# Retention attention and two feed-forward stages: where in the program weights are converted

## The chip, the core and the metric

The kernel runs on one core of one Trainium2 chip. What is measured is the device time of one execution in microseconds (us). The program has 17,896 profiled instructions on five engines: TensorE (PE, with its weight loads as PEld), VectorE (DVE), ScalarE (ACT), GpSimd (POOL) and SyncE (SP), which issues the transfers.

## What is computed

```python
def _attn_ref(q, k, v):                        # 4 x 8 heads, 576 positions, 64 wide
    scores = scale * np.matmul(q, k.transpose(0, 1, 3, 2))
    ret = scores * Dmat[None, :, :, :]         # gamma ** distance, causal
    return np.matmul(ret, v)

x = attn_out as 2304 tokens x 512
h = x @ w_in                                   # 512 x 2048
g = np.maximum(h, 0.0) ** 2
x = g @ w_out                                  # 2048 x 512
p = domain_probs / (domain_probs.sum(-1, keepdims=True) + 1e-09)
for e in range(4):                             # 4 experts, 512 x 1024 x 512
    h = np.maximum(x @ w1[e], 0.0)
    out += p[:, e:e + 1] * (h @ w2[e])
```

## The kernel before

**Number format.** Every float32 operand of the feed-forward stages is split into a high and a low part in a reduced float32 type, and a product is three matmuls: high by high, high by low, low by high. Making the parts is a *conversion*: ScalarE casts the high part, and another engine subtracts it for the low part. For a weight this is the helper `split` (ScalarE line 124, POOL line 125); the first stage's weights come in 64-bit floats and go through `from_f64` (lines 87 to 121), which for each piece of 128x256 runs one ScalarE operation, five on VectorE, then one on ScalarE and two on POOL.

**Chunks and groups.** The hidden width is cut into chunks c of 256. Chunks 0 to 7 belong to the dense stage (`NW1 = 8`), 8 to 23 to the experts over token groups 0, 1 and 4, and 24 to 39 to the experts again, over groups 2 and 3. Groups 0 to 3 have 512 tokens and group 4 has 256. A job is a chunk with one group or with a pair of groups. `layer1` (line 460) or `layer1_pair` (line 494) makes the hidden values of a job, `layer2_1` (line 613) or `layer2_2` (line 645) multiplies them by the second weight, one job behind. `layer1_pair` computes two groups with seven block products in place of eight: a *set* of 42 matmuls in the order A11, S2, S3, A12, S1, A22, S4, with sums on VectorE between them (line 501). Its fourth product adds to the bank of the first, and may start only when ScalarE has copied that bank (line 507).

**Input blocks.** A pair reads seven prepared input blocks (slots 0 to 6 of `xh`, `xl`). `slots` prepares them from `y` in three generators: `parts` casts a half on ScalarE (line 573) and takes the low part (line 574) of the first half on VectorE and of the second on POOL; `minus` forms differences on VectorE (line 581). Generators `sa` serve groups 0 and 1 ahead of chunk 8, `sb` serve groups 2 and 3 ahead of chunk 24.

**Banks.** All matmul results of the feed-forward stages rotate through eight PSUM banks, so a result can be started only when the one eight places earlier has been read: by line 619 on ScalarE (chunk 0), 621 on VectorE, or 653 on VectorE.

**What sets the order of the work around the change.** Each engine's instructions run in the order in which the Python code issues them. Conversions are generators in a list `work`; `tick(n)` advances the first of them by n steps, and is called in the attention (line 419), after each half of `layer1` (469) and after each tile of `layer2` (622, 656). `pace[0]` is the number of steps (line 690). `drain` runs a generator to its end where its result is needed. `queue_weights` (line 204) puts the next weights into `work` in a fixed order as their buffers come free: `split_w1` and `split_w2` of chunk c, each with two buffers. A weight of chunks 0 to 7 takes 28 steps, a later `split_w1` 12 or 11 and a later `split_w2` 4. Raw weights arrive through three buffers (`wraw`, line 43) in pieces of 256 KB; `load_piece` issues the next load when a piece has been converted, on SP's queue, which also carries the attention's inputs and the output.

The attention runs 16 units of two steps each. Steps of conversion begin in unit 3.

Of the kernel before, what the change touches and what calls it, by code (L numbers as in the profile page):

```python
# [26 lines left out]
NW1, NW2 = 8, 16  # L27
# [6 lines left out]
def tile_kernel(ctx, tc, qT, kT, kn, vn, v4d, mask, qdec, kdec, wd, w, probs, out):  # L34
    nc = tc.nc
# [165 lines left out]
    splits = {}  # L201
    free = {(f, c) for f in (split_w1, split_w2) for c in range(2)}

    def queue_weights(*place):
        free.update(place)
        while order and order[0] in free:
            f, c = order.pop(0)
            splits[f, c] = f(c)
            work.append(splits[f, c])


    def attention(a):
# [181 lines left out]
        for i, s in enumerate(steps):  # L394
            n, h = s
            nxt = steps[i + 1] if i + 1 < len(steps) else None
            un, uc = (n, 2) if h == 0 else (n + 1, 0)
            update(un, uc)
            if nxt:
                scores(nxt)  # L400
                masked(nxt)
            cs = CS[h]
            for c in cs[:-1]:
                inner(s, c)
            update(un, uc + 1)
            inner(s, cs[-1])
            for c in cs:
                if c:
                    outer(s, c)
            finish(s)  # L410
            if h == 0:
                prepare(n + 2)
            else:
                load(n + 3)
            if h == 0 and n in (1, 2, 3):
                load_piece()
            if s == (3, 0):
                queue_weights()
            tick(1 + h)

    with tc.manual_schedule():
        with ExitStack() as a:
# [18 lines left out]
        pace = [2]  # L441
# [36 lines left out]
                out=lo, in0=h, scalar=0.0, in1=f32(hi), op0=ALU.max, op1=ALU.subtract  # L478
            )

        def layer1_pair(c, ga, gb):


            w1h, w1l = w1s[c]
            (ha, la), (hb, lb) = hidden(ga), hidden(gb)
            bank = lambda: ps.tile([128, GT], F32, name="h", tag="ps")
            v = nc.vector

            def product(o, i, j, first=True):

                n = 0
                for k in range(2):
                    for a, x in ((w1h, xh_), (w1h, xl_), (w1l, xh_)):
                        nc.tensor.matmul(  # L494
                            o, a[:, i, k, :], slot(x, j)[:, k, :], start=(first and n == 0), stop=(n == 5),
                            skip_group_check=True,
                        )
                        n += 1

            def add(o, x, y):  # L500
                v.tensor_tensor(out=o, in0=x, in1=y, op=ALU.add)  # L501

            u = [tp.tile([128, GT], F32, name="r") for _ in range(2)]
            u.append(cvp.tile([128, GT], F32, name="cv_tp"))
            b1 = bank()
            product(b1, A11, 0)
            nc.scalar.copy(out=u[0], in_=b1)  # L507
            b6 = bank()
            product(b6, S2, 3)
            add(u[1], b6, u[0])  # L510
            b7 = bank()
            product(b7, S3, 2)
            add(u[2], b7, u[1])
            product(b1, A12, 4, False)
            relu_split(b1, ha[:, 0, :], la[:, 0, :])
            b5 = bank()
            product(b5, S1, 1)
            add(u[2], b5, u[2])
            product(b7, A22, 5, False)
            add(u[0], b7, u[1])  # L520
            relu_split(u[2], hb[:, 1, :], lb[:, 1, :])
            product(b5, S4, 6, False)
            add(u[1], b5, u[1])
            relu_split(u[0], ha[:, 1, :], la[:, 1, :])
            relu_split(u[1], hb[:, 0, :], lb[:, 0, :])
            gh[c, ga], gl[c, ga] = ha, la
            gh[c, gb], gl[c, gb] = hb, lb
# [37 lines left out]
                op0=ALU.mult, op1=ALU.mult,  # L565
            )

        def parts(i, src):

            for k in range(2):  # L570
                yield
                hi = slot(xh_, i)[:, k, :]
                nc.scalar.copy(out=hi, in_=src[:, k, :])
                (nc.gpsimd if k else nc.vector).tensor_tensor(
                    out=slot(xl_, i)[:, k, :], in0=src[:, k, :], in1=f32(hi), op=ALU.subtract
                )

# [5 lines left out]
        def slots(ga, gb):  # L583
# [2 lines left out]
            b11, b21 = yacc[ga][:, :2, :], yacc[ga][:, 2:, :]  # L586
            b12, b22 = yacc[gb][:, :2, :], yacc[gb][:, 2:, :]

            def first():
                yield from parts(0, b11)  # L590
                yield from minus(b11, b12, b11)
# [4 lines left out]
                yield from parts(2, b12)  # L596

            def second():
                yield from parts(4, b21)
                yield from minus(b21, b21, b11)  # L600
                yield from parts(5, b21)

            return first(), second(), parts(6, b22)

        def layer2_1(c, g):
            w2h, w2l = w2s[c]
# [24 lines left out]
        def layer2_2(c, g):  # L631
# [7 lines left out]
            for m in range(GS[g] // 128):  # L639
# [12 lines left out]
                else:  # L652
                    nc.vector.scalar_tensor_tensor(  # L653
                        out=acc, in0=o, scalar=pr[:, tt, e : e + 1], in1=acc, op0=ALU.mult, op1=ALU.add
                    )
                tick(2)
                if last:
                    nc.sync.dma_start(out=out[tt * 128 : (tt + 1) * 128, :], in_=acc)

# [25 lines left out]
        for i, job in enumerate(jobs):  # L685
# [1 line left out]
            g = scaled.get(c)  # L687
            drain(splits[split_w1, c])

            pace[0] = 6 if i < 3 else 3 if c in (p, q) else 2  # L690
            if job in ((NW1, (0, 1)), (NW1 + NW2, (2, 3))):
                drain((sa if c == NW1 else sb)[2])
            if g and gs == (0, 1):
                for k in range(KT):
                    magnitude(g, k, rest[k])
            if len(gs) > 1:
                layer1_pair(c, *gs)
            elif job == (p, (4,)):
                s = layer1(c, *gs, lambda: scale(1, mags[1]))
                rescale(1, s)  # L700
                work.insert(0, sa[0])
            else:
                layer1(c, *gs)
# [92 lines left out]
```

## Time and profile before

| | before |
|---|---|
| median of 3 runs | 1269.1 us (1267.95 to 1269.91) |
| the profiled execution | 1268.69 us, its span 1266.9 us |
| PE busy | 1231.6 us, 97% |
| PEld busy | 1031.9 us, 81% |
| VectorE, ScalarE, POOL busy | 832.1, 452.5, 537.2 us |
| granted TensorE clock, mean | 0.993 |

The span is what the trace covers, from the first to the last instruction; 1.8 us of the execution lie around it. A busy share of PE counts overlapping matmuls and so hides short idle stretches; the timeline shows these with the engine that ended each. In a group of the lines view the numbers behind the bar are the busy time, the mean duration of one instruction, and the idle time before them.

### The profile page before, as it was taken

What the parts mean: (1) busy time and instruction counts of PE and PEld (TensorE: products, weight loads), DVE (VectorE), ACT (ScalarE), POOL (GpSimd) and SP (SyncE); (2) the same over time, 40 slices, a digit from 0 to 9 for tenths busy, and PEclk for the clock granted to TensorE, in tenths of its full rate; (3) what the DMA queues carried; (4) which work ended last, traced back from release to release, by engine and by line L of the source; (5) the groups of instructions that cost most, each with busy time, mean ns of one, the idle gap of its engine ahead of it and who ended that gap; (6) DMA issues with size and microseconds to landing.
All of it is one profiled execution on the core that took longest, in us unless ns stands there. A gap on an engine that the chain in (4) does not pass through costs nothing.

```text
span 1266.9 us, 17896 instructions
## 1 busy us (share of the span) xinstructions
PE 1231.6 (97%) x6576; PEld 1031.9 (81%) x6576; DVE 832.1 (66%) x1400; ACT 452.5 (36%) x1109; POOL 537.2 (42%) x641
## 2 busy tenths in 40 slices
PE   7998999999999996999999999999989999999998
PEld 6886788888888885888888888888868888888887
DVE  3767577777777686355765675656855676767665
ACT  3544533333333334433332322323434333333330
POOL 3655545454455349323442233422353434434340
PEclk9999999999999999999999999999999999999999
DMA  9832111111111001110111111110031101111111
GB/s 326 285 105 67 42 42 42 42 50 35 41 50 44 32 1 34 50 34 34 51 42 42 34 34 50 42 42 34 17 133 51 67 34 67 43 58 51 51 42 66
DMA packets 41303, 76.31 MB, mean 60 GB/s; under 512 B 4864, under 2 KB 5888, under 8 KB 41216
## 3 DMA queue, kind: packets, MB, share of 16 engines
q1 hardware_dynamic: 40704, 74.47, 17.3%
q8 instruction: 51, 0.84, 0.3%
q10 hardware_dynamic: 512, 0.70, 0.2%
q14 instruction: 36, 0.29, 0.1%
HBM read 70.44 MB, written 4.72 MB: 59 GB/s over the span
## 4 chain that ended last, share of the span: by engine, by line
PE 59%; DMA 0%; ACT 0%; POOL 0%; issue 0%; DVE 0%; DVEq 0%; POOLq 0%; ACTq 0%
PE o L645 31%; PE h L494 24%; PE h L460 4%; DMA wraw<-w 0%; PE o L613 0%; PE sm L537 0%; POOL w1lo L125 0%; PE po L554 0%; ACT w1hi L124 0%; POOL w2lo L125 0%; ACT r L507 0%; ACT w2hi L124 0%; DVE oacc L653 0%; DVE r L501 0%; DVE cv_m L158 0%
## 5 line engine op out<-in xcount | busy, mean ns | idle before, releaser
L653 DVE SCALAR_TENSOR_TENSOR oacc<-o,pr,oacc 128x512 f32<-128x512 f32 x270 | 197.1, 744 | 41.7 <-PE o L645 41.3
L645 PE MATMUL o<-w2hi,ghi 128*128 128x512 f32 x576 | 224.5, 390 | 0.0
L645 PE MATMUL o<-w2hi,glo 128*128 128x512 f32 x576 | 224.2, 389 | 0.0
L645 PE MATMUL o<-w2lo,ghi 128*128 128x512 f32 x576 | 224.1, 389 | 0.0
L494 PE MATMUL h<-xh,w1hi 128*128 128x512 f32 x448 | 176.7, 394 | 10.9 <-ACT r L507 8.9
L125 POOL TENSOR_TENSOR w2lo<-wraw,w2hi 128x256 fp32r<-128x256 f32 x128 | 94.1, 763 | 219.0 <-ACT w2hi L124 219.0
L494 PE MATMUL h<-xh,w1lo 128*128 128x512 f32 x448 | 175.9, 393 | 1.8 <-POOL w1lo L125 1.8
L494 PE MATMUL h<-xl,w1hi 128*128 128x512 f32 x448 | 176.0, 393 | 0.0
L125 POOL TENSOR_TENSOR glo<-r,ghi 128x512 fp32r<-128x512 f32 (+1 forms) x80 | 96.2, 1203 | 148.3 <-ACT ghi L124 147.8
L460 PE MATMUL h<-xh,w1hi 128*128 128x512 f32 (+1 forms) x448 | 154.6, 345 | 3.6 <-ACT y L619 2.8
L460 PE MATMUL h<-xl,w1hi 128*128 128x512 f32 (+1 forms) x448 | 154.0, 344 | 0.0
L460 PE MATMUL h<-xh,w1lo 128*128 128x512 f32 (+1 forms) x448 | 153.9, 344 | 0.0
L125 POOL TENSOR_TENSOR w1lo<-wraw,w1hi 128x256 fp32r<-128x256 f32 x112 | 89.3, 797 | 123.0 <-ACT w1hi L124 123.0
L501 DVE TENSOR_TENSOR r<-h,r 128x512 f32<-128x512 f32 x96 | 66.4, 691 | 103.9 <-PE h L494 95.7
L645 PEld LDWEIGHTS o<-w2lo,ghi 128*128 128x128 f32 x576 | 108.1, 188 | 22.5
L645 PEld LDWEIGHTS o<-w2hi,ghi 128*128 128x128 f32 x576 | 108.2, 188 | 22.0
L645 PEld LDWEIGHTS o<-w2hi,glo 128*128 128x128 f32 x576 | 108.2, 188 | 22.0
L613 PE MATMUL o<-glo,w2hi 128*128 128x512 f32 (+1 forms) x320 | 119.0, 372 | 4.8 <-POOL glo L125 4.8
L613 PE MATMUL o<-ghi,w2hi 128*128 128x512 f32 (+1 forms) x320 | 119.0, 372 | 2.7 <-ACT y L619 1.7
L613 PE MATMUL o<-ghi,w2lo 128*128 128x512 f32 (+1 forms) x320 | 118.4, 370 | 0.0
L494 PEld LDWEIGHTS h<-xh,w1hi 128*128 128x128 f32 x448 | 85.1, 190 | 30.6 <-ACT r L507 9.7
L465 DVE TENSOR_TENSOR r<-r 128x512 f32<-128x512 f32 (+1 forms) x80 | 58.5, 731 | 76.6 <-ACT r L464 76.4
(97 smaller groups left out, 2100.2 us busy)
## 6 DMA issues: line engine op xcount, KB each, us to landing
wraw<-w SPq DMA_DIRECT2D x128, 256.0 KB, 2.7
wraw<-wd SPq DMA_DIRECT2D x64, 256.0 KB, 2.7
q_t<-qT SPq DMA_DIRECT2D x16, 288.0 KB, 4.2
out<-oacc SPq DMA_DIRECT2D x18, 256.0 KB, 2.0
kt<-kT SPq DMA_DIRECT2D x15, 288.0 KB, 5.1
v_n<-vn SPq DMA_DIRECT2D x16, 256.0 KB, 4.3
k_n<-kn SPq DMA_DIRECT2D x15, 256.0 KB, 4.8
qd<-qdec SPq DMA_DIRECT2D x4, 224.0 KB, 4.9
```

What stands on the lines that cost most here:

```text
L125: nc.gpsimd.tensor_tensor(out=lo, in0=src, in1=f32(hi), op=ALU.subtract)
L460: nc.tensor.matmul(h, wk(a, f, k), x[:, k, :], start=(n == 0), stop=(n == 3 * KT - 1))
L465: nc.vector.tensor_tensor(out=r, in0=r, in1=r, op=ALU.mult)
L494: nc.tensor.matmul(o, a[:, i, k, :], slot(x, j)[:, k, :], start=(first and n == 0), stop=(n == 5), skip_group_check=True,)
L501: v.tensor_tensor(out=o, in0=x, in1=y, op=ALU.add)
L613: nc.tensor.matmul(o, a[:, f, 128 * m : 128 * m + 128], x[:, f, :], start=(n == 0), stop=(n == 3 * FT - 1))
L645: nc.tensor.matmul(o, a[:, f, 128 * m : 128 * m + 128], x[:, f, :], start=(n == 0), stop=(n == 3 * FT - 1))
L653: nc.vector.scalar_tensor_tensor(out=acc, in0=o, scalar=pr[:, tt, e : e + 1], in1=acc, op0=ALU.mult, op1=ALU.add)
```

## The change

In the attention every step of a unit is followed by two conversion steps (one and two before), and the first three jobs no longer run at six steps a place. Three weights are *held* out of `work`: the second weight of chunk 8 and the first weight of chunk 9 until the first set has been issued, and the first weight of chunk 25 until the set of chunk 24 is about to be issued; that one is then advanced between products of this set, three steps at each of four places. The low parts of the last three slots are taken wholly on VectorE. In `layer2_2` the pace holds in place of a fixed 2, and it is 4 in the jobs of chunk 23 (`z`).

```diff
+    held = {(split_w2, NW1), (split_w1, NW1 + 1), (split_w1, NW1 + NW2 + 1)}
+
     def queue_weights(*place):
         free.update(place)
-        while order and order[0] in free:
+        while order and order[0] in free and order[0] not in held:
...
             if s == (3, 0):
                 queue_weights()
-            tick(1 + h)
+            tick(2)
...
-        def layer1_pair(c, ga, gb):
+        def layer1_pair(c, ga, gb, steps=0):
...
             product(b1, A12, 4, False)
+            tick(steps)
             relu_split(b1, ha[:, 0, :], la[:, 0, :])
             b5 = bank()
             product(b5, S1, 1)
+            tick(steps)
             add(u[2], b5, u[2])
             product(b7, A22, 5, False)
+            tick(steps)
             add(u[0], b7, u[1])
             relu_split(u[2], hb[:, 1, :], lb[:, 1, :])
             product(b5, S4, 6, False)
+            tick(steps)
...
-        def parts(i, src):
+        def parts(i, src, engines=(nc.vector, nc.gpsimd)):
...
-                (nc.gpsimd if k else nc.vector).tensor_tensor(
+                engines[k].tensor_tensor(
...
+            late = (nc.vector, nc.vector)
...
-                yield from parts(4, b21)
+                yield from parts(4, b21, late)
                 yield from minus(b21, b21, b11)
-                yield from parts(5, b21)
-
-            return first(), second(), parts(6, b22)
+                yield from parts(5, b21, late)
+
+            return first(), second(), parts(6, b22, late)
...
-                tick(2)
+                tick(pace[0])
...
-            pace[0] = 6 if i < 3 else 3 if c in (p, q) else 2
+            pace[0] = 3 if c in (p, q) else 4 if c == z else 2
...
-                layer1_pair(c, *gs)
+                if job == (NW1 + NW2, (2, 3)):
+                    held.clear()
+                    queue_weights()
+                layer1_pair(c, *gs, steps=3 if job == (NW1 + NW2, (2, 3)) else 0)
+
+                if job == (NW1, (0, 1)):
+                    held.difference_update({(split_w2, NW1), (split_w1, NW1 + 1)})
+                    queue_weights()
```

TensorE's own instructions keep their order throughout. Three places of other engines are shown as the programs list them. The changed file is longer, so its line numbers differ: ScalarE's copy is line 507 before and 509 now, `layer1_pair`'s sums 501 and 503, its relu 476 and 478, the low parts of the slots 574 and 580, their differences 581 and 587, the evictions of `layer2_2` 653 and 661.

The first place is ScalarE ahead of the first set (chunk 8, groups 0 and 1): the last hidden values of chunk 7 (`r`, `ghi`), the last slot's casts (`xh`), and the copy on which the set's fourth product waits. Before:

```order
L573 CAST xh<-y_1332 128x512 x2
L124 CAST w1hi<-wraw 128x256
L124 CAST w1hi<-cv_d 128x256
L124 CAST w1hi<-cv_m 128x256
L124 CAST w1hi<-wraw 128x256
L124 CAST w1hi<-cv_m 128x256
L507 COPY r<-h 128x512
```

Now:

```order
L579 CAST xh<-y_1359 128x512 x2
L509 COPY r<-h 128x512
L478 ACTIVATE ghi<-h 128x512
L478 ACTIVATE ghi<-cv_tp 128x512
L478 ACTIVATE ghi<-r 128x512 x2
L124 CAST w2hi<-wraw 128x256 x4
L124 CAST w1hi<-wraw 128x256
```

Five casts of chunk 9's first weight no longer stand ahead of the copy; chunk 8's second weight and chunk 9's first follow the set's last relu.

The second place is VectorE while `layer2` of chunk 22 runs over groups 0 and 1 (eight tiles, evicted to `oacc`) and the slots of groups 2 and 3 are prepared (`xl`, and `y` for the differences). Before, the first tiles:

```order
L653 SCALAR_TENSOR_TENSOR oacc_5264<-o_8474,pr,oacc_5264 128x512
L574 TENSOR_TENSOR xl<-y_1333,xh 128x512
L653 SCALAR_TENSOR_TENSOR oacc_5264<-o_8484,pr,oacc_5264 128x512
L581 TENSOR_TENSOR y_1333<-y_1334,y_1333 128x512
L653 SCALAR_TENSOR_TENSOR oacc_5264<-o_8495,pr,oacc_5264 128x512
L581 TENSOR_TENSOR y_1333<-y_1334,y_1333 128x512
L574 TENSOR_TENSOR xl<-y_1333,xh 128x512
L653 SCALAR_TENSOR_TENSOR oacc_5264<-o_8506,pr,oacc_5264 128x512
```

Now the second to the fourth tile:

```order
L661 SCALAR_TENSOR_TENSOR oacc_5240<-o_8487,pr,oacc_5240 128x512
L587 TENSOR_TENSOR y_1360<-y_1361,y_1360 128x512
L580 TENSOR_TENSOR xl<-y_1360,xh 128x512
L587 TENSOR_TENSOR y_1361<-y_1361 128x512
L661 SCALAR_TENSOR_TENSOR oacc_5240<-o_8501,pr,oacc_5240 128x512
L587 TENSOR_TENSOR y_1361<-y_1361 128x512
L587 TENSOR_TENSOR y_1360<-y_1361,y_1360 128x512 x2
L580 TENSOR_TENSOR xl<-y_1360,xh 128x512
L661 SCALAR_TENSOR_TENSOR oacc_5240<-o_8514,pr,oacc_5240 128x512
```

Between two evictions stand two to four operations of the slots, where one or two stood. Counted over the whole listing, eighteen of them now stand ahead of the seventh eviction, nine before.

The third place is VectorE in the set of chunk 24 and behind it. Before, from the set's last sum on:

```order
L501 TENSOR_TENSOR r<-h,r 128x512
L477 SCALAR_TENSOR_TENSOR glo<-r,ghi 128x512 x2
L653 SCALAR_TENSOR_TENSOR oacc_5431<-o_8821,pr,oacc_5431 128x512
L653 SCALAR_TENSOR_TENSOR oacc_5431<-o_8834,pr,oacc_5431 128x512
L158 TENSOR_TENSOR cv_m<-wraw 128x256
L158 TENSOR_TENSOR cv_d<-cv_m,wraw 128x256
L158 TENSOR_TENSOR cv_m<-wraw 128x256
L158 TENSOR_TENSOR cv_d<-wraw,cv_d 128x256
```

Now, from the low part of the set's first finished result on:

```order
L479 SCALAR_TENSOR_TENSOR glo<-h,ghi 128x512
L158 TENSOR_TENSOR cv_m<-wraw 128x256
L503 TENSOR_TENSOR cv_tp<-h,cv_tp 128x512
L158 TENSOR_TENSOR cv_d<-cv_m,wraw 128x256
L158 TENSOR_TENSOR cv_m<-wraw 128x256
L503 TENSOR_TENSOR r<-h,r 128x512
L479 SCALAR_TENSOR_TENSOR glo<-cv_tp,ghi 128x512
L158 TENSOR_TENSOR cv_d<-wraw,cv_d 128x256
L503 TENSOR_TENSOR r<-h,r 128x512
```

The four operations on chunk 25's raw weight (`cv_m`, `cv_d`) stood behind the set and the evictions that follow it, and stand now between the set's sums.

## Rows read from the trace of the kernel before

**Rows 1.** The page: busy time, share of the span and instructions of each engine.
```profile
PE 1231.6 (97%) x6576; PEld 1031.9 (81%) x6576; DVE 832.1 (66%) x1400; ACT 452.5 (36%) x1109; POOL 537.2 (42%) x641
```

**Rows 2.** The chain that ended last, in order of time: start, us, what.
```profile
513.50 5.44 PE o L613 x24
518.94 2.87 PE h L460 x24
...
532.72 9.52 PE h L494 x42
```

**Rows 3.** Timeline of PE: start, us, engine, line, names, count [idle before, who ended it].
```profile
82.84 0.50 PE L460 MATMUL h<-xh,w1hi 128*128 128x512 f32 x1 [0.84 <-DVE xl L375]
...
140.83 0.39 PE L460 MATMUL h<-xh,w1hi 128*128 128x512 f32 x1
```

**Rows 4.** Waits of PE between 82 and 141 us: total, times, longest.
```profile
PE h L460 <- ACT y L619: 2.8, 4, 0.9
```

**Rows 5.** Windows: busy us (instructions) of PE, PEld, DVE, ACT, POOL; granted clock; DMA.
```profile
135.00:139.00 4.00, 4.00 (x13) 3.10 (x12) 1.50 (x4) 2.67 (x8) 1.47 (x2) 0.57 0.02 4
...
505.00:511.00 6.00, 5.88 (x14) 4.64 (x15) 2.43 (x5) 0.67 (x2) 1.37 (x2) 0.52 0.13 44
```

**Rows 6.** Timeline of PE around the first set.
```profile
474.43 0.28 PE L613 MATMUL o<-ghi,w2hi 128*128 128x256 f32 x1
...
484.19 0.39 PE L613 MATMUL o<-ghi,w2hi 128*128 128x512 f32 x1
...
487.86 0.50 PE L613 MATMUL o<-glo,w2hi 128*128 128x512 f32 x1 [2.55 <-POOL glo L125]
...
505.12 0.80 PE L494 MATMUL h<-xh,w1hi 128*128 128x512 f32 x1 [7.51 <-ACT r L507]
...
513.34 0.39 PE L613 MATMUL o<-ghi,w2hi 128*128 128x512 f32 x1
```

**Rows 7.** Timeline of PE around the set of chunk 25.
```profile
936.07 0.39 PE L645 MATMUL o<-w2hi,ghi 128*128 128x512 f32 x1
...
955.76 0.39 PE L645 MATMUL o<-w2hi,ghi 128*128 128x512 f32 x1
```

**Rows 8.** The chain that ended last, around the set of chunk 25.
```profile
939.67 3.01 DMA wraw<-w
...
946.33 2.59 DMA wraw<-w
```

**Rows 9.** Timeline of PE in the attention, the first outer products of units 1, 4 and 15.
```profile
18.61 0.39 PE L352 MATMUL xo<-q_s,st 128*64 128x128 f32 x4
...
31.65 0.50 PE L352 MATMUL xo<-q_s,st 128*64 128x128 f32 x6
...
80.44 0.50 PE L352 MATMUL xo<-q_s,st 128*64 128x128 f32 x6
```

**Rows 10.** Timeline of POOL ahead of the first set.
```profile
483.01 1.29 POOL L125 TENSOR_TENSOR glo<-r,ghi 128x512 fp32r<-128x512 f32 x1
484.26 1.87 POOL L125 TENSOR_TENSOR w2lo<-wraw,w2hi 128x256 fp32r<-128x256 f32 x2
```

**Rows 11.** Timeline of ACT ahead of the copy that the first set waits for.
```profile
499.39 0.40 ACT L124 CAST w1hi<-wraw 128x256 fp32r<-128x256 f32 x1
...
504.49 0.58 ACT L507 COPY r<-h 128x512 f32<-128x512 f32 x1
```

**Rows 12.** Timeline: first tile of chunk 22's `layer2`, its eviction.
```profile
896.27 0.39 PE L645 MATMUL o<-w2hi,ghi 128*128 128x512 f32 x1
...
898.48 0.74 DVE L653 SCALAR_TENSOR_TENSOR oacc<-o,pr,oacc 128x512 f32<-128x512 f32 x1
```

**Rows 13.** Timeline of DVE: two low parts of slots, without and with POOL at work.
```profile
909.80 0.68 DVE L574 TENSOR_TENSOR xl<-y,xh 128x512 fp32r<-128x512 f32 x1
...
911.09 1.38 DVE L574 TENSOR_TENSOR xl<-y,xh 128x512 fp32r<-128x512 f32 x1
```

**Rows 14.** Lines view of DVE from 898 to 918 us, the slots of groups 2 and 3.
```profile
L574 DVE TENSOR_TENSOR xl<-y,xh 128x512 fp32r<-128x512 f32 x6 | 5.3, 888 | 0.4 <-ACT xh L573 0.4
```

## The prediction

> **What bounds the kernel now.** The page comes first: TensorE is busy 97% of the span, VectorE, the next, 66% [rows 1]. TensorE's instructions keep their order in this change, so the time can move only by what TensorE waits for and by its clock. Next comes the chain that ended last, which gives the undisturbed price of each block: 24 matmuls of 512 columns take 5.44 us (0.227 each), 24 of 256 columns 2.87, and a set of 42 takes 9.52 [rows 2]. Then I read the timeline for stretches that last longer than these prices say. There are three.
>
> *Place A*, the first jobs. From 82.84 to 140.83 [rows 3] 57.99 us pass; the stretch holds 192 matmuls of 512 columns (43.5 us) and 24 of 256 (2.9), 46.4 in all. Excess 11.6. The waits there are many and short, above all 2.8 us for ScalarE to read a bank (line 619) [rows 4], and the granted clock falls to its lower level, 1.2 GHz, for most of four microseconds (mean 0.57) [rows 5]. Six conversion steps at each place load VectorE, ScalarE and POOL with more than they can do beside these jobs.
>
> *Place B*, the first set. From 474.43 to 513.34 38.91 us pass [rows 6] for 90 matmuls of 512 columns and 24 of 256, 20.4 + 2.9 = 23.3. Excess 15.6. Two waits make most of it: 2.55 for POOL's low part and 7.51 for the copy of line 507 [rows 6]; behind the second the clock stands at the lower level (0.52 over 505 to 511) [rows 5].
>
> *Place C*, the set of chunk 25. From 936.07 to 955.76 [rows 7] 19.69 us pass for 54 matmuls, 12.2. Excess 7.4. The chain shows why: two loads of raw weights, 3.01 and 2.59 us, stand on the path one behind the other [rows 8].
>
> Together 34.6 us, so a kernel without any of it would stand at 1234. The sum below is made against the profiled execution, 1268.7; the median of the runs is 0.4 higher, which I neglect.
>
> **The change part by part.**
>
> *Attention, 13 more steps.* From unit 3 on, 26 steps of the attention get 2 conversion steps each, 52 in place of 39. The first weight takes 28, so 24 of the second weight's 28 are now done there and the other 4 in the first job. Two more raw pieces are loaded there, on SP's queue between the inputs; inputs are asked for three units ahead, some 13 us, which hides a load. If that lead were gone, each would cost about the 3 us of [rows 8]. The price of the steps: units 1 to 3 last (31.65 − 18.61) / 3 = 4.35 us each, units 4 to 14, with three steps in each, (80.44 − 31.65) / 11 = 4.44 [rows 9]. So three steps cost 0.09 a unit, and 13 more about 0.4. They now also stand ahead of the longer mask multiplication, and I take **+0.7**, with 0 and 2.5 as ends (2.5 is 0.19 for each of the 13, twice what a unit's three steps cost now).
>
> *Place A, pace 2.* The first three jobs' six `layer1` places and the eight tiles behind them issue 28 steps in place of 84. That is the pace of the jobs behind 140.83, where I see no wait. Eight tiles last 10.9 us (48 times 0.227), and the eight banks give ScalarE that much slack. Nothing new is late: the second chunk's first weight needs 32 steps by the sixth job and gets 52, its second weight 60 by the seventh and gets 64. I leave 0.4 of the 11.6: **−11.2** (ends −11.6 and −8; the poor end is another dip of the clock, 1.7 us, and two thirds of the 2.8 of rows 4).
>
> *Place B.* Three things leave the path. POOL begins the first of two low parts at 483.01 and then, from 484.26, does two parts of chunk 8's second weight (1.87 us) before the other [rows 10]. With that weight held, the other ends at 485.6, or 486.2 if a VectorE operation gets in between; the 2.55 becomes about 1.1 with the restart. Second, three low parts of slots (about 1.29 us each on POOL, the size of the low part in rows 10) go to VectorE, and the other parts of the second weight go too, so what ScalarE does ahead of the copy moves forward. Third, the casts from 499.39 to the copy at 504.49 go [rows 11], 5.1 us. The copy would come at 499.4 by that alone, and about 2 us sooner by the other two: I take 497.4. The set starts when the 24 matmuls ahead of it end, 484.19 [rows 6] + 5.4 + 1.1 = 490.7, and its fourth product is due 18 matmuls (4.1) later, at 494.8. So it waits 2.6 for the copy. Next in line is VectorE: three evictions and two moved low parts stand ahead of the set's sums, and the sixth product waits for them; I put one low part, 0.7. From 474.43 to 484.19 [rows 6] pass 1.4 us more than the 8.3 that the 48 matmuls need, which nothing touches. So the residue is 1.1 + 2.6 + 0.7 + 1.4 = 5.8, and the excess falls by **−9.8** (ends −13, where the copy is in time, and −5, where it comes at 499.4 and the clock dips again). The held weights come later: chunk 8's second weight is needed 8.3 us behind the set (5.44 + 2.87), and its four casts and low parts take some 4; chunk 9's first has 10.9 us more. Both are hidden; if not, 3 us of a load appear.
>
> *Place C, the split in the set.* Chunk 24's second weight (4 steps) and eight of the eleven steps of chunk 25's first weight now stand between the products. The raw piece that these need is asked for about 4 us into the set and lands 3 us later [rows 8], while the sixth product is about to run. VectorE's first operation on it stands ahead of the sum for the seventh product, which waits about 0.3. The last raw piece lands some 15.2 us behind the start of chunk 24's set, the copy of the next set follows 0.9 later, and that set's fourth product is due at 9.5 + 2.7 + 4.1 = 16.3: another 0.3. So **−6.8** (ends −7.4 and −3, one load late).
>
> *Place C, pace 4.* The slots of groups 2 and 3 are now pushed onto VectorE within six tiles. Ahead of the seventh eviction stand six evictions and 18 slot operations (in the order listing). VectorE begins the first eviction at 898.48, the tiles begin at 896.27 [rows 12]. To the end of the seventh these are 25 operations at about 0.68 [rows 13], 17.0; with 0.7 lost to each of four POOL operations (1.38 against 0.68) 19.8, so 918.3. Its bank is needed by the fifth of the next eight tiles, 10.9 + 2.9 + 5.4 = 19.2 behind 896.27, at 915.5. **+2.8** (ends 0 and +5; 0 if POOL's work overlaps less, 5 if all ten low parts take 1.38). What is queued behind it on VectorE, chunk 24's first weight, has until that chunk's set.
>
> *Moved low parts.* A low part on VectorE took 0.68 us alone and 1.38 while POOL worked [rows 13], 0.89 in the mean of that stretch [rows 14]; the terms above hold these. The Trainium skill, SBUF — State Buffer, section "Who interferes with whom", says that a VectorE instruction with two SBUF inputs contends with a GpSimd instruction that reads SBUF, and that the loser is blocked for the whole of the other. By that rule the move speaks against itself while POOL is busy. The trace agrees on the kind, with the 0.70 by which 1.38 exceeds 0.68. As a mechanism of this kernel it is the first rival.
>
> **Sum.** 0.7 − 11.2 − 9.8 − 6.8 + 2.8 = −24.3, so 1268.7 − 24.3 = **1244.4 us**.
>
> **The rivals.**
>
> 1. *New waits on VectorE take the place of the old.* The moved low parts and the evictions queue behind POOL's operations. At place B two low parts take 0.7 more each, the three evictions come after them (2.0), and the sixth product waits 3.4 more; at place C the stall is 2.5 longer. 24.3 − 5.9 = 18.4: 1250.3. For it: a low part already takes 0.89 in the mean [rows 14]. Against: POOL loses the same low parts and the held weights.
> 2. *All the cover holds.* Copy in time, banks free, no new stall: −11.6 − 12.9 − 7.2 + 0.3 = −31.4, 1237.3. For it: all three places lose the casts and low parts that burden them. Against: VectorE is loaded ahead of chunk 24.
> 3. *The attention pays.* Each of 13 steps holds up its mask multiplication and TensorE by about 0.9: 11.7, place A's gain given back, 1255.4. Against: three steps a unit cost only 0.09 now [rows 9].
> 4. *Slower: the held weights never catch up.* If each later chunk's first weight were still being converted when its set begins, every set would wait as the one of chunk 25 did, 7.4 us. There are 31 sets behind the first; from the fourth late one on (4 × 7.4 = 29.6 against 24.3) the kernel would be slower, and with ten it stands at 1268.7 − 24.3 + 74 = 1318. Against: a chunk needs 16 steps and gets 24 at pace 2, so a lag of 16 steps is gone after two chunks.
>
> **How the numbers follow.** The forecast 0.60, rival 1 0.20, rival 2 0.12, rival 3 0.05, rival 4 0.03. The range runs from 1237.0 (rival 2) to 1252.0 (rival 1 with 1.7 more); it leaves out rivals 3 and 4 and the tails, less than 2 in 10. A measurement of this kernel can tell about 0.2%, 2.5 us, from no change. All cases but the fourth are faster by far more: faster 0.95, same 0.02, slower 0.03.
>
> **What would show it.** Right: in the timeline no bank wait for `y` in the first jobs and a full clock there; the copy of the first set ahead of the second weight's casts, with a wait of 1 to 4 us in place of 7.51; TensorE waiting for VectorE's evictions in the second eight tiles ahead of chunk 24's set, where it did not; no load of raw weights on the chain around chunk 25's set. Wrong: units of the attention longer than 4.6 us, sets of chunks 9 to 11 with waits for `w1hi` or `w1lo`, or a lower clock behind the first set.

## Result, and the profile after the change

| | before | after |
|---|---|---|
| median of the runs | 1268.73 us (1267.95 to 1269.91) | 1252.08 us (1251.64 to 1253.96) |
| ratio | 1 | 0.9871, 95% interval 0.9854 to 0.9888 |
| the profiled execution, its span | 1268.69, 1266.9 | 1251.88, 1250.1 |

The median is 1.3% shorter. The forecast of 1244.4 starts from the profiled execution and is 7.5 us below the one measured, 1251.88; the median lies 0.1 above the upper end of the range, 1252.0. The page of the changed kernel, against [rows 1]:

```profile
span 1250.1 us, 17901 instructions
PE 1223.1 (98%) x6576; PEld 1027.6 (82%) x6576; DVE 840.6 (67%) x1406; ACT 452.4 (36%) x1109; POOL 526.2 (42%) x635
PEclk9999999999999999999999999999999999999999
```

No slice falls below 9 tenths of the clock. The timeline of PE gives the start of each stretch, as [rows 3], [rows 6] and [rows 7] did for the kernel before:

```profile
87.67 0.50 PE L462 MATMUL h<-xh,w1hi 128*128 128x512 f32 x1 [1.31 <-DVE xl L377]
134.26 0.39 PE L462 MATMUL h<-xh,w1hi 128*128 128x512 f32 x1
467.87 0.28 PE L621 MATMUL o<-ghi,w2hi 128*128 128x256 f32 x1
497.72 0.39 PE L621 MATMUL o<-ghi,w2hi 128*128 128x512 f32 x1
880.65 0.39 PE L653 MATMUL o<-w2hi,ghi 128*128 128x512 f32 x1
914.56 0.39 PE L496 MATMUL h<-xh,w1hi 128*128 128x512 f32 x1
924.34 0.39 PE L653 MATMUL o<-w2hi,ghi 128*128 128x512 f32 x1
938.95 0.39 PE L653 MATMUL o<-w2hi,ghi 128*128 128x512 f32 x1
```

The difference between two neighbours is the length of a stretch. The rows of 914.56 and 924.34 bound the set of chunk 24. The same subtraction on the trace of before gives the table (us). The stretches left out, 333.6, 382.9 and 311.1 long, have the same length in both to 0.01.

| stretch | before | after | difference | predicted |
|---|---|---|---|---|
| attention, to the first job | 82.84 | 87.67 | +4.83 | +0.7 |
| place A, first jobs | 57.98 | 46.59 | −11.39 | −11.2 |
| place B, first set | 38.91 | 29.85 | −9.06 | −9.8 |
| tiles of chunks 22 and 23 (pace 4) | 30.28 | 33.91 | +3.63 | +2.8 |
| set of chunk 24, set of chunk 25 behind it | 29.21 | 24.39 | −4.82 | −6.8 |
| sum | | | −16.81 | −24.3 |

The spans differ by 16.8, so nothing is missing. Of the 7.5 us, 4.1 are the attention, 2.0 the split, 0.8 pace 4 and 0.7 place B, less 0.2 at place A. What PE waits for now (total, times, longest; a first row, for the first `kt`, which the kernel before has too, and the waits of 0.3 are left out):

```profile
PE h L496 <- ACT r L509: 3.8, 2, 2.0
PE xo L342 <- DVE pt L304: 3.5, 4, 1.3
PE o L653 <- DVE oacc L661: 2.7, 3, 1.6
PE o L621 <- POOL glo L125: 1.6, 3, 0.7
PE state L318 <- DVE k_n L272: 1.4, 1, 1.4
PE h L462 <- DVE xl L377: 1.3, 1, 1.3
PE state L318 <- ACT st L326: 1.2, 2, 0.6
PE state L318 <- POOL k_n L272: 1.2, 1, 1.2
PE h L496 <- DVE cv_tp L503: 1.2, 1, 1.2
```

The wait for `y` of [rows 4] is gone. In the attention, the second row (3.5 us, for the longer mask) and the wait for POOL's `k_n` are new: before, PE waited in the attention, from 20 us on, for nothing but the last `xl`, 0.8. With that last wait, now 1.3, the new waits come to 3.5 + 1.2 + 0.5 = 5.2, which is the +4.83 and a little more.

Where the mask is late, the timelines between 41 and 47 us show why. TensorE's first product with the mask's result, and VectorE:

```profile
45.41 0.66 PE L342 MATMUL xo<-pt,v_n 128*64 128x128 f32 x8 [0.92 <-DVE pt L304]
42.06 0.56 DVE L377 TENSOR_TENSOR xl<-xo,xh 128x384 fp32r<-128x384 f32 x1 [0.58 <-ACT xh L375]
42.54 0.67 DVE L112 TENSOR_SCALAR cv_tp<-cv_m 128x256 int32<-128x256 int32 x1
43.24 1.24 DVE L114 SCALAR_TENSOR_TENSOR cv_b<-wraw,cv_tp 128x256 f32<-128x256 uint32 x1
44.41 0.94 DVE L304 TENSOR_TENSOR pt<-qk,mk 128x768 f32<-128x768 f32 x1
```

POOL in the same stretch of the changed kernel, its preparation of the next unit:

```profile
42.02 1.04 POOL L272 TENSOR_TENSOR k_n<-k_n,kd 128x512 f32<-128x512 f32 x1 [3.01 <-DMA k_n<-kn]
43.02 1.18 POOL L274 TENSOR_TENSOR q_s<-q_t,qd 128x448 f32<-128x448 f32 x1
```

Both conversion steps that now stand ahead of the longer mask (line 304) run beside POOL's preparation. L114 ends at 44.48, 0.28 behind POOL's `q_s`, and the mask multiplication starts 1.9 us behind the start of the first of the two; PE waits 0.92 for it, until 45.41. By form, over 30 to 82 us, L114 took in the kernel before

```profile
L114 DVE SCALAR_TENSOR_TENSOR cv_b<-wraw,cv_tp 128x256 f32<-128x256 uint32 x5 | 2.1, 427 | 0.1
```

and in the changed one

```profile
L114 DVE SCALAR_TENSOR_TENSOR cv_b<-wraw,cv_tp 128x256 f32<-128x256 uint32 x6 | 5.3, 880 | 0.2
```

The mean is 427 ns there, and now 880. The Trainium skill, SBUF — State Buffer, section "Who interferes with whom", has the loser of such a contention blocked for the whole of the other instruction; the end of L114 just behind the end of `q_s` agrees with that. All the traces of this case go the same way. In the 14 of them L114 begins 429 times while a POOL instruction is running, and each time it ends 0.28 to 0.33 us behind that one's end. The other 467 times it takes 0.41 to 0.43, also in the 197 where POOL starts beside it. So what counts is whether POOL has begun first: it had for one of five L114 in the attention of the kernel before, and for five of seven in the changed one.

### The profile page after: what moved, and what is told of

Same layout as the page of the kernel before. It is cut to its first block, busy times and chain, and to the rows that moved or that the text cites. A ratio compares the mean times of both kernels' runs of the same rounds, so it can differ in the third digit from the quotient of the medians.

```text
span 1250.1 us, 17901 instructions
## 1 busy us (share of the span) xinstructions
PE 1223.1 (98%) x6576; PEld 1027.6 (82%) x6576; DVE 840.6 (67%) x1406; ACT 452.4 (36%) x1109; POOL 526.2 (42%) x635
## 3 DMA queue, kind: packets, MB, share of 16 engines
q1 hardware_dynamic: 40704, 74.47, 17.5%
## 4 chain that ended last, share of the span: by engine, by line
PE 90%; DVE 5%; ACT 2%; DMA 1%; issue 1%; POOL 1%; ACTq 0%; POOLq 0%; DVEq 0%; SPq 0%
PE o L653 30%; PE h L496 24%; PE h L462 18%; PE o L621 14%; PE xo L342 1%; DVE xl L580 1%; PE qk L290 1%; DMA k_n<-kn 1%; PE xo L354 1%; DVE y L587 1%; PE state L318 1%; DVE y L553 1%; DVE r L467 1%; ACT xh L579 1%; DVE y L629 0%
## 5 line engine op out<-in xcount | busy, mean ns | idle before, releaser
L653 PE MATMUL o<-w2hi,ghi 128*128 128x512 f32 x576 | 224.8, 390 | 2.7 <-DVE oacc L661 2.7
L661 DVE SCALAR_TENSOR_TENSOR oacc<-o,pr,oacc 128x512 f32<-128x512 f32 x270 | 197.1, 745 | 42.5 <-PE o L653 41.9
L653 PE MATMUL o<-w2hi,glo 128*128 128x512 f32 x576 | 224.3, 389 | 0.0
L653 PE MATMUL o<-w2lo,ghi 128*128 128x512 f32 x576 | 224.1, 389 | 0.0
L653 PEld LDWEIGHTS o<-w2hi,ghi 128*128 128x128 f32 x576 | 108.2, 188 | 26.0 <-DVE oacc L661 4.0
L653 PEld LDWEIGHTS o<-w2lo,ghi 128*128 128x128 f32 x576 | 108.1, 188 | 22.6
L653 PEld LDWEIGHTS o<-w2hi,glo 128*128 128x128 f32 x576 | 108.2, 188 | 21.7
L467 DVE TENSOR_TENSOR r<-r 128x512 f32<-128x512 f32 (+1 forms) x80 | 63.8, 798 | 69.8 <-ACT r L466 69.6
```

The costliest lines, as they stand in the source:

```text
L467: nc.vector.tensor_tensor(out=r, in0=r, in1=r, op=ALU.mult)
L653: nc.tensor.matmul(o, a[:, f, 128 * m : 128 * m + 128], x[:, f, :], start=(n == 0), stop=(n == 3 * FT - 1))
L661: nc.vector.scalar_tensor_tensor(out=acc, in0=o, scalar=pr[:, tt, e : e + 1], in1=acc, op0=ALU.mult, op1=ALU.add)
```

## Experiments

Each is an edit of the changed kernel. All but the last two have one time each, beside the kernel before on the same chip, so a difference of a few us is read from the length of its stretch, not from the time. The attention is the stretch that varies most between kernels that don't touch it: its end lay at 88.22, 88.27, 88.36 and 90.37 in four of them, 87.67 in the profile above. So the +4.83 is the lowest of five traces with the same order in the attention; the highest is +7.5.

**Who pays for the attention's steps: one ahead of the longer mask, three ahead of the shorter** (52 steps, as changed).

```diff
-            tick(2)
+            tick(1 if h == 0 else 3)
```

> The changed kernel with one conversion step after the first half of a unit and three after the second (two and two in the change), so the same 52 steps in the attention, but again one ahead of the longer mask multiplication. Theory (place): the attention lost 4.8 us because two steps stand ahead of the longer mask; the first feed-forward matmul, at 82.84 us before and 87.67 in the change, comes back to 83 to 84, TensorE's four waits for the mask (3.5 us) go, and the time is about 1248. Rival (amount): 13 more steps cost what they cost wherever they stand; the first feed-forward matmul stays at 87 to 88 and the time at 1252.

Measured 1251.12 us; the first job starts at 85.13. The waits of PE between 20 and 85.3 us:

```profile
PE state L318 <- ACT st L326: 1.7, 2, 1.2
PE h L462 <- DVE xl L377: 0.8, 1, 0.8
PE xo L342 <- DVE pt L306: 0.4, 2, 0.2
PE xo L342 <- DVE pt L304: 0.2, 1, 0.2
```

Half of the loss is gone: with one step ahead of the longer mask it is late by 0.2 in all, and `k_n` isn't late. The other 2.3 us stay. ScalarE's state copies are late now: its first operation on a piece (line 102), which waits for the L114 before it, queues ahead of them. So the place of a step decides whom it delays. The time fell by less than the attention did, since in this run the lower clock stood for 3.4 us at the set of chunk 25 (stretch 16.22 in place of 14.61).

**POOL's preparation moved to the unit's second half.**

```diff
-            if h == 0:
+            if h == 1:
                 prepare(n + 2)
-            else:
                 load(n + 3)
```

> The changed kernel with POOL's preparation of a unit (two multiplications, 2.2 us) issued after the second half of a unit in place of the first; the conversion steps stay two and two. Theory (two steps, and POOL at work beside them): the waits for the longer mask come only where POOL's preparation runs beside the two steps and doubles their length; without it TensorE's waits for the longer mask fall from 3.5 us to under 1, and the first feed-forward matmul comes to 84 to 85.5. Rival (the two steps alone are too long): the waits stay at 3 us or more, and it stays at 87 to 88.

Measured 1258.0 us, first job at 90.68. It doesn't tell the two apart. POOL waits for the load of `k_n` or for TensorE, and its work still ran beside the steps ahead of the longer mask (mask waits 2.8 in 4; POOL had begun first for five of seven L114); besides, PE waited 2.0 for `k_n`, and the granted clock stood at the lower level for 7 us behind that.

**Pace 2 behind chunk 23.**

```diff
-            pace[0] = 3 if c in (p, q) else 4 if c == z else 2
+            pace[0] = 3 if c in (p, q) else 2
```

> The changed kernel with pace 2 in place of 4 in the jobs of chunk 23. Theory: the 2.7 us in which TensorE waits for VectorE's evictions ahead of chunk 24's set (3.2 us with the restarts) come from the pace alone and go; from the first tile of chunk 22's layer2 to the first matmul of chunk 24's set, 33.91 us in the change, pass 30.4 to 30.9; the time is about 1249. Rival: the slots come later at this pace, and the set of chunk 24 waits for a slot by as much as the evictions gave back; the time stays within a microsecond of 1252.

Measured 1249.39 us. The tiles last 911.64 − 881.36 = 30.28, to the hundredth what they took before, against 33.91, and the row "PE o L653 <- DVE oacc L661" is gone. Pace 4 cost 3.63 and gave nothing that shows: the stretch of chunks 24 and 25 is 24.66 (24.39 with pace 4).

**Four steps instead of three between the products of chunk 24's set** (which the expectations of the combinations below call chunk 25's).

```diff
-                layer1_pair(c, *gs, steps=3 if job == (NW1 + NW2, (2, 3)) else 0)
+                layer1_pair(c, *gs, steps=4 if job == (NW1 + NW2, (2, 3)) else 0)
```

> The changed kernel with four conversion steps at each of the four places in the set of chunk 24 (three in the change), so that the whole first weight of chunk 25 is converted inside that set. Theory: the last raw piece is then asked for some 2 us earlier, and the wait for the copy in the set of chunk 25 (2.0 us, at 933) falls below 0.5; the time is about 1250. Rival: the steps delay VectorE's sums of the set, so what is gained at the copy is lost inside the set of chunk 24, which takes 11 us or more in place of 9.78; the time stays at 1252 or rises.

Measured 1251.45 us. The set of chunk 24 takes 10.65 (9.78), the stretch behind it 12.26 (14.61): 1.5 us less in all. 12.26 is the undisturbed price of its 54 matmuls (12.2): the load is no longer on the path. In the changed kernel it was, as the chain of waits shows, against the two loads of [rows 8]:

```profile
927.22 1.37 PE h L496 x6
...
928.65 0.55 POOL w1lo L125
929.20 2.86 DMA wraw<-w
...
933.33 5.78 PE h L496 x24
```

The piece is asked for at 929.20, 4.9 us behind the end of chunk 24's set. Its buffer comes free with the casts that stand behind the set's last `ghi` on ScalarE, and with POOL's low part of them, which the chain shows just ahead of the load (changed kernel):

```profile
926.72 0.63 ACT L478 ACTIVATE ghi<-r 128x512 fp32r<-128x512 f32 x1 [1.45 <-DVE r L503]
927.25 0.39 ACT L124 CAST w1hi<-wraw 128x256 fp32r<-128x256 f32 x1
...
932.09 0.71 ACT L124 CAST w2hi<-wraw 128x256 fp32r<-128x256 f32 x2 [2.90 <-DMA wraw<-w]
932.70 0.58 ACT L509 COPY r<-h 128x512 f32<-128x512 f32 x1
```

and that `ghi` waits for the set's sums, between which VectorE does conversions of up to 0.96 us beside POOL's low parts. But the load also stands behind a store of the output on SP's queue, and this store waits 5.5 us for its eviction on VectorE (line 661):

```profile
928.76 0.34 SPq L666 DMA_DIRECT2D out<-oacc  x1
929.20 1.23 SPq L84 DMA_DIRECT2D wraw<-w  x2
```

With four steps both loads are issued ahead of that store, the first of them 12.2 us behind the start of chunk 24's set in place of 14.6. So the gain can come from the sooner buffer or from the place on the queue, and no run separates them.

**Two steps ahead of the longer mask, one ahead of the shorter** (39 steps, the number before).

```diff
-            tick(2)
+            tick(2 - h)
```

> The changed kernel with 2 steps ahead of the longer mask multiplication and 1 ahead of the shorter (39 steps in the attention, the number of the kernel before, but the other way round). Theory (the price is the place: a second step ahead of the longer multiplication runs beside POOL's preparation of the next unit and delays the mask): TensorE still waits about 3 us for the masks, and the first job starts between 86 and 88. Rival (the price is the number of steps, 52 against 39): the mask waits stay under 1.2 us and the first job starts at 82.5 to 83.5, as before. Place A: a few steps of the first weight chunk's second weight are left to be drained after the third job, so 46.6 to 49.

Measured 1265.76 us, first job at 91.66: neither theory. The mask waits are 1.2, but two units last 8.90 and 7.68 us for another reason. SP's queue in this run:

```profile
32.98 0.33 SPq L255 DMA_DIRECT2D v_n<-vn  x1
38.65 0.33 SPq L81 DMA_DIRECT2D wraw<-wd  x1
39.08 0.37 SPq L248 DMA_DIRECT2D q_t<-qT  x1
...
42.62 1.04 SPq L254 DMA_DIRECT2D k_n<-kn  x1
```

The raw piece waits until 38.65 for its buffer, whose last reader is L114, and two units' inputs stand behind it on the queue and go out together. PE waits 1.96 for `k_n` at 47.46, and behind that the clock falls (windows, this run):

```profile
48.00:54.00 6.00, 6.00 (x62) 5.31 (x62) 2.76 (x5) 2.01 (x11) 4.74 (x6) 0.52 0.77 244
```

Place A was longer too (52.35), with waits for the second weight, as in the first combination below, and the stretch behind it lasted 337.47 in place of 333.61, with a wait of 1.9 for a later second weight. The run leaves number against place open, and shows a second way in which steps cost the attention: raw pieces that hold up its inputs.

**No hold at the first set.**

```diff
-    held = {(split_w2, NW1), (split_w1, NW1 + 1), (split_w1, NW1 + NW2 + 1)}
+    held = {(split_w1, NW1 + NW2 + 1)}
```

> The changed kernel without the hold at the first seven-product set: the second weight of chunk 8 and the first of chunk 9 join the queue as soon as their buffers are free, as before; all else as changed. Theory (the hold carries place B: about 5.1 us of casts and 1.5 us of POOL work stand ahead of the copy otherwise): place B lasts 35 to 38 us in place of 29.85, with a wait of 4 to 7 us for the copy of line 509 and the lower clock behind it; the time rises to 1257 to 1260. Rival (the three low parts moved to VectorE are enough by themselves): place B under 32, time under 1254.

Measured 1261.16 us. Place B takes 38.27, nearly the 38.91 of before, with

```profile
498.59 0.80 PE L496 MATMUL h<-xh,w1hi 128*128 128x512 f32 x1 [7.74 <-ACT r L509]
```

in place of the 7.51 of [rows 6], and half the clock behind it (0.50 over 499 to 503). So the hold is worth 8.4 of the 9.1 us.

**The low parts of slots 4 to 6 back on POOL.**

```diff
-            late = (nc.vector, nc.vector)
+            late = (nc.vector, nc.gpsimd)
```

> The changed kernel with the low parts of slots 4 to 6 back on POOL where they were (every second one), all else as changed. Theory of the prediction (the moved low parts bring the copy of the first set forward by up to 2 us, and cost one low part, 0.7, on VectorE): place B 30.5 to 32 in place of 29.85, the wait for the copy 3 to 4 in place of 1.9, the wait of the sixth product for VectorE gone. Rival (VectorE is what the set waits for, the move costs more than it gives): place B 28.5 to 29.8. At the tiles behind chunk 23 (33.91 now, 30.28 before) fewer operations stand ahead of the seventh eviction: 31 to 33.

Measured 1254.17 us (its first job starts at 90.37). Place B 30.10, with a wait of 1.9 for the copy and none for `cv_tp`. Ten runs that leave place B alone gave 29.80 to 30.08, so the move is worth nothing that can be told there. That the wait for `cv_tp` is gone is not the move's doing: in this run the clock falls behind the wait for the copy (0.57 over 494 to 498), and in the five runs above and below where it falls there too, that wait is missing as well. The tiles of chunks 22 and 23 take 33.05: the move cost 0.9 of pace 4's 3.6.

**A first combination**: 39 steps, one ahead of the longer mask, with pace 3 in the first three jobs, pace 2 behind chunk 23, and four steps.

```diff
-            tick(2)
+            tick(1 + h)
...
-            pace[0] = 3 if c in (p, q) else 4 if c == z else 2
+            pace[0] = 3 if c in (p, q) or i < 3 else 2
...
-                layer1_pair(c, *gs, steps=3 if job == (NW1 + NW2, (2, 3)) else 0)
+                layer1_pair(c, *gs, steps=4 if job == (NW1 + NW2, (2, 3)) else 0)
```

> A version put together from what the runs so far showed: 1 step ahead of the longer mask multiplication and 2 ahead of the shorter (39 in all, as before the change), pace 3 in the first three jobs so that the 17 steps of the first second weight that are then left fit into their six places, pace 2 in the tiles behind chunk 23, four steps between the products of chunk 25's set. Theory (the number of steps that the attention had before costs it nothing, and the rest of place A's gain stays): first job at 82.8 to 83.5, place A 46.5 to 48, the tiles behind chunk 23 30.3, the set and stretch of chunk 25 22.9 together; time 1242 to 1245. Rival (without 13 steps done in the attention place A is lost again): place A 50 to 55, time 1247 to 1252.

Measured 1246.44 us. The first job starts at 82.34: without the 13 steps the attention pays nothing, and no mask is late. But place A takes 51.58. Its waits:

```profile
PE o L621 <- POOL w2lo L121: 1.8, 1, 1.8
PE h L462 <- DVE xl L377: 0.8, 1, 0.8
PE o L621 <- ACT w2hi L119: 0.6, 1, 0.6
```

The last piece of the first second weight is ready at 105.87, too late by 1.85, and the clock falls behind that (0.72 over 105 to 111). No bank is waited for at pace 3. So part of place A's gain came with the steps put into the attention, but not all of it.

**The pairs of steps behind the mask** (50 steps).

```diff
                 scores(nxt)
                 masked(nxt)
+            tick(2)
             cs = CS[h]
...
-            tick(2)
```

> The changed kernel with each pair of the attention's conversion steps issued behind the next mask multiplication instead of ahead of it (50 steps in the attention, two places ahead of long and short masks alike; the steps still meet POOL's preparation). Theory (the attention's +4.83 is the time by which two steps, lengthened by POOL, hold up the mask that TensorE waits for): the waits for masks vanish (under 0.5 us), though the two last operations of a conversion still take more than 0.7 us in the mean; the first job starts at 83 to 84.7, time 1247.5 to 1249.5. Rival (the engines behind pay all the same, ScalarE's state copies and the evictions come late): the first job starts at 86 to 88, time as changed, 1251 to 1253.

Measured 1250.59 us, first job at 86.14, the lower end of the rival's range, but not for its reason. Waits between 20 and 86.3 us:

```profile
PE state L318 <- POOL k_n L272: 2.8, 1, 2.8
PE h L462 <- DVE xl L377: 1.3, 1, 1.3
PE state L318 <- ACT st L326: 0.2, 1, 0.2
```

No mask is late, although L114 still takes 729 ns in the mean. All units from the second on but two last 4.34 or 4.35, under the 4.44 that the prediction worked out from [rows 9]; one of the two lasts 4.77, the other 7.38, with the wait of 2.8 for `k_n`, whose load stands on SP's queue behind a raw piece that waited 5.3 for L114. So it is shown that the first cost is the steps' delay of the mask. The inputs are next in line.

**Second combination**: 42 steps, one ahead of the longer mask, queued a unit earlier, pace 4, 3, 3 in the first jobs.

```diff
-            if s == (3, 0):
+            if s == (2, 0):
...
-            tick(2)
+            tick(1 + h)
...
+            pace[0] = 4 if i == 0 else 3 if c in (p, q) or i < 3 else 2
```

> The combination of before (1 step ahead of the longer mask, 2 ahead of the shorter; pace 2 behind chunk 23; four steps between the products of chunk 25's set), with the first weights queued one unit earlier (42 steps in the attention) and pace 4 in the first job, 3 in the next two, so that the 14 steps left of the first second weight are done a job before it is needed. Theory (in the combination with 39 steps the last raw piece was converted just in time: 1.85 us for its low part and a fall of the clock behind it): first job at 82.3 to 83.0, place A 46.5 to 48, time 1241 to 1243.5. Rival (any pace above 2 in the first jobs brings the bank waits and the lower clock back): place A 50 to 53, time 1245 to 1248.

Measured 1243.69 us: first job at 83.38, place A 47.83, with 1.0 left of the wait for `w2lo`.

**Third combination, steps behind the mask**: 41 steps, pace 4 in the first two jobs.

```diff
+            tick(1 + h)
             cs = CS[h]
...
-            tick(2)
...
+            pace[0] = 4 if i < 2 else 3 if c in (p, q) else 2
```

> The combination once more (first weights queued one unit earlier, pace 2 behind chunk 23, four steps between the products of chunk 25's set), with the attention's steps, 1 and 2 by turns, 41 in all, behind the next mask multiplication, and pace 4 in the first two jobs, 2 from the third on, so that the 15 steps left of the first second weight are done in four places. Theory (behind the mask a step costs TensorE nothing, and fewer steps keep the raw pieces from holding up the inputs on SP's queue): no wait for a mask, no wait of 2.8 for k_n, units of 4.34, first job at 82.0 to 82.8; place A 46.5 to 47.2 as the last raw piece is ready in time; time 1239.5 to 1242. Rival (the wait for k_n comes with steps behind the mask, whatever their number): first job at 84 to 86, time 1243 to 1246.

Measured 1246.73 us (1244.57 to 1247.43), ratio 0.9832 (0.9815 to 0.985). Place A is 46.59, but two waits for `k_n` (2.3 together) put the first job at 85.45: the rival holds, fewer steps don't remove that wait.

**The same with the steps ahead of the mask**, 42 in all.

```diff
-            if s == (3, 0):
+            if s == (2, 0):
...
-            tick(2)
+            tick(1 + h)
...
+            pace[0] = 4 if i < 2 else 3 if c in (p, q) else 2
```

> The same with the steps ahead of the mask multiplication as in the changed kernel, 1 ahead of the longer and 2 ahead of the shorter, 42 in all. Theory: as the run with 42 steps before, first job at 82.3 to 83.5, but place A 46.5 to 47.2 in place of 47.83, since the second weight is done a job before its use; time 1241 to 1243. Rival (pace 4 in the second job fills the banks' readers, ScalarE above all): waits for y or ghi of over 1 us, place A 48 to 52, time 1244 to 1248.

Measured **1242.56 us** (1241.76 to 1243.58) against 1268.21 for the kernel before: ratio **0.9798** (0.9783 to 0.9814). The changed kernel's is 0.9871 (0.9854 to 0.9888), so this order beats it as well, by some 9.5 us. First job at 83.65, place A 46.59, tiles 30.28, the two sets 22.91. Its waits up to 83.8 us:

```profile
PE h L462 <- DVE xl L377: 0.9, 1, 0.9
PE state L318 <- POOL k_n L272: 0.3, 1, 0.3
```

## Why the prediction failed, point by point

- **Attention, +0.7: the step that failed.** It measured +4.83, beyond the upper end of 2.5, and up to +7.5 in the other runs with this order. The sign of being wrong that the prediction had named came too: five units last 5.03 to 5.74 us, over 4.6. The prediction took "three steps cost 0.09 a unit" [rows 9] and carried it on to four. That price came from an order in which only one step stood ahead of the longer mask, where it had room. A second step there has none where POOL's preparation has begun first: L114 then takes up to 1.24 in place of 0.43. The prediction saw the place ("they now also stand ahead of the longer mask multiplication") and put 0.3 on it. It priced contention with POOL for the moved low parts alone, not for these steps. Rival 3 named the mechanism, and assumed 0.9 for each of 13 places; four paid, 0.6 to 1.3 each. With one step there (the first, eighth and last runs) or the steps behind the mask (the ninth) the mask waits fall to 0.6 or less. The load lead of 13 us was also trusted too far: `k_n` cost 1.2, and up to 2.8 in other orders. That raw pieces on SP's queue cause that wait fits the rows of two runs, but no run varied it alone.
- **Place A, −11.2: right** (−11.39), with no wait left but the first `xl` and a full clock. The reason was half told: the eighth run shows that the second weight must also be ready well ahead of its first use.
- **Place B, −9.8: right in size** (−9.06), and by the part named as largest: the hold is 8.4 of it. The copy began 22.2 us behind the start of place B (490.03 − 467.87), against 23.0 in the working; the set waits 1.8 for it (2.6 predicted) and 1.2 for VectorE (0.7). That the moved low parts bring the copy forward isn't borne out: with them back on POOL it began 22.3 us behind.
- **Place C, the split, −6.8: too much by 2.0.** One load stayed on the path. The working let the last raw piece land 15.2 us behind the start of chunk 24's set; it landed at 932.1, 17.5 behind. The two small waits were 0.26 and 2.0 in place of 0.3 each. Four steps instead of three give 1.5 back. Whether the buffer or the store ahead of it on SP's queue held the load up stays open.
- **Place C, pace 4, +2.8: right in kind**, +3.63 in size; undone alone, it goes wholly.
- **Rival 1** gave 1250.3, nearer the time, but the loss was not where it put it: at place B VectorE holds the set up by 1.2, not by 3.4 more. **Rival 4** didn't come: the stretches behind the places kept their length to 0.01 us, so the held weights caught up.

## What to carry to other kernels

A price of background steps read off at three a unit is a price of their places and not of their number alone. Both count: with one step ahead of the longer mask, 39 steps put the first job at 82.34, 42 at 83.38 and 83.65, and 52 at 85.13. Before adding a step, look at what stands next behind it on its engine, how much room that has, and what the neighbouring engine does just then. Background work pays as long as it stands ahead of something with slack and the transfers it triggers don't stand ahead of the main loop's inputs on the same queue. Put a weight's conversion off until the first set's copy is issued (8.4 us here), but give what is needed soonest a lead of a whole job.

## What was not expected of the hardware

- VectorE's conversion operations depend on POOL more than a mean shows, and what they lose can be told from the trace. If POOL is already running when L114 begins, it ends 0.28 us (the median of 429) behind POOL's end; the slots' low parts on 128x512 end 0.55 behind (the median of 128). If POOL starts later or not at all, they take 0.41 to 0.43 and 0.67 to 0.70.
- VectorE's instructions that read a PSUM bank show nothing of this. The longer mask multiplication took at most 0.96 us with POOL at work at its start (103 times) and without (121 times), and the evictions of `layer2_2` at most 0.75 in all traces. So the mask itself isn't slowed, only the step ahead of it.
- Waits of about 2 us at the same instruction were sometimes followed by the lower clock and sometimes not. At chunk 25's set the changed kernel waited 2.03 with the clock full behind it, while the first two experiments, with waits of 2.04 and 2.21, ran behind them at a mean of 0.57 and 0.63 for four microseconds (stretches of 16.22 and 16.37 in place of 14.61). In the attention a wait of 1.96 for `k_n` was followed by six microseconds at 0.52, and one of 2.8 in the ninth experiment by none (clock 1.00 over 60 to 72). At the first set the wait for the copy, 1.75 to 1.88 us in the 12 traces with the hold, was followed in six of them by the lower clock (mean 0.72 over six microseconds); place B lasted 30.00 to 30.10 in these, and 29.80 to 29.87 in the others. What tells them apart stays open.
